# An attention and two-layer kernel on one core: w_in loaded in two pieces of eight column chunks, and the order of the first third of the work arranged anew

## The chip, the cores and the metric

The kernel runs on one core of one Trainium2 chip. The metric is the time of one execution on the device in microseconds (us), lower is better. The engines are called as in the profile: PE (TensorE, matrix products and transposes), DVE (VectorE), ACT (ScalarE), POOL (GpSimd) and SP (SyncE, which issues most of the transfers).

## The reference

A causal attention in which every query looks at the six best of 24 key chunks alone, and on its output two matrix products with an ELU between them:

```python
batch, n_heads, seq, head_dim = (4, 8, 768, 64)
chunk = 32; top_k = 6; scale = 1 / sqrt(64)
k_min, k_max = k_chunks.min(axis=3), k_chunks.max(axis=3)
ub = sum(maximum(q * k_min, q * k_max), axis=-1)          # a bound for each query and chunk
ub = where(causal, ub, -1e9)
top_chunks = argsort(ub, axis=-1)[..., -top_k:]
scores = where(selected & causal, scale * q @ k.T, -1e9)
attn = exp(scores - max) ; attn = attn / (sum(attn) + 1e-09)
x = (attn @ v) as [3072, 512]                              # tokens x (heads * 64)
h = x @ w_in                                               # w_in 512 x 2048
g = where(h > 0, h, exp(minimum(h, 0)) - 1)
out = g @ w_out                                            # w_out 2048 x 512
```

## The kernel before

The 3072 tokens are eight units of 384. Units 0 and 1 hold the first 192 tokens (tags with "p") and the next 192 (tags with "s") of batches 0 and 1 together; units 2 to 7 are the later half rows of batches 0 and 1 and the halves of batches 2 and 3. For each unit the kernel prepares keys and queries, selects chunks (not for the first 192 tokens, where all chunks are allowed), forms scores and attention, and turns the result into xt, four tiles of 128 channels x 384 tokens. Then comes that unit's layer.

The work is recorded as small steps with their reads and writes (`Graph`), and two long strings, ORDER and PLACES, give the order in which the steps are emitted, the engine of each one, and the buffer (one of 8 PSUM banks, one of 11 "f" buffers for loaded rows, and so on) of each tile. Nothing is rearranged afterwards: every engine, and every queue of transfers, goes through its steps in the order of that string, and waits in place where an input or a buffer is not ready.

The steps that the text below names:

- ldk, ldq, ldv (L304, issued by SP, two of ldk by ACT): loads of keys, queries and values. ldq0s00 and ldq0s10 are the two loads of queries for batch 0, unit "s", ldk0s00 and ldk0s10 those of its keys. Their rows are 64 floats, 256 bytes. ec (SP): a copy of a constant into the keys' tile.
- kT, qT (L402, PE): transposes of loaded rows into a bank, four of 96 x 128 each; kmin, kmax (L367, DVE) and ks0, ks1 (L370) make the bounds of chunks from them; kt, qt, qh, ka, qa (L320 on ACT, L322 on DVE and POOL) copy them on, qr (L344 and L342) is a ReLU of a query.
- tr, sc, ex, pv, rcp, on: mask, scores, exponential, product with values, reciprocal and division. ub, ubT, max, lt, sT, mk: the selection.
- px (L669, PE) and xt (L320 on ACT, L322 on DVE): the turned result, the layer's input.
- w_in0 and so on (L291), w_out0 to w_out3 (L297): the weights, loaded by POOL with a cast from float32 to bfloat16.
- h (L851, PE, four products of 128 x 384 for each of 16 column chunks), e (ACT, exponential), m (L860, POOL or DVE), g (DVE): the first product and the ELU. h0.4 is chunk 4 of unit 0; it needs all four xt and the piece of w_in that holds column chunk 4. o (L875, PE): the second product.
- vz, rz, oh, kq, tris, es: constants; kb, ky202: parts of keys' tiles for later batches.

On POOL the pieces stand in this order among the rest: oh, vz0, ka01p0, v0p1, rz, w_in1 (column chunks 4 to 7), v0p0, v1p0, w_in0 (chunks 0 to 3), ka10p0, ks1p1, w_in2 (chunks 8 to 15), and then with work between them w_out0 to w_out3. The layer of unit 0 starts with chunks 4, 6 and 5 accordingly, then qT0s0, chunk 3, qT0s1, chunks 2, 1, 7, the selection's ub00, chunk 0, and the upper eight.

A load of w_in is one call:

```python
def load_w_in(i, c0, c1):
    return g.op(f"w_in{i}", (POOL,),
                lambda e: nc.gpsimd.dma_start(out=w_in_sb[:, :, P * c0:P * c1],
                                              in_=wi[:, :, P * c0:P * c1]),
                writes=[(fixed, ("wi", fc)) for fc in range(c0, c1)], dma=True)
```

Its rows in the core's memory are 128 bfloat16 for each column chunk: 1 KB in the pieces of four chunks, 2 KB in the piece of eight.

Of the kernel before, what the change touches and what calls it, by code (L numbers as in the profile page):

```python
# [39 lines left out]
G0iS0WD01A02D09D06S0sG0kD0jG0aS0yD03D00D0qG0mG0bA0VG04D05G0eS0uG0cG0dA0tS0rS0vS0xD0lD0oS0wS0YS0X  # L40
P0MD0OD0QS0BP1oP0DP1aP11S0ZS0zD0ED0NA0HA0IG0fG0gD0FP0KP1pA1eG0pP1kA0LD1bP0TA0RA15A17G16P1jP1tP1l
S0+D0UP1qP1uD1cP18A1nD13S2gS2fG0CA1rP1hD19A1sG0nP1zD12S2hS2iP1yA1iP1AA1gA1mGmED0PA1CP1vA1xA1BG0A
P1DP26P25P1ED10G0-S2PS2vS2OD27D28D1FA1wP1YP20P2aGmDA0SP29D2bP1XA2cP1+D21G0JP1IP1OP1RP1SP1HS2IP2o
P1ND1GD1JD1ZD1KP2dG1dGmFA1-P1LD2qD1PA1QD2jD22P23D1TD1UD2eA2sD24A1MS2QP1VD1WG08G2uG0hP2BD2DD2CA2t
Pm-Pn6G2EAn7GbsGmGPn2Gn8D2pG2rAm+Dn0D14D0GAn3Dn4P2wPmWA2xA2yS2RP2JA2KDn5D2zPmSPmODn9Dn1AmXAmTD2L
GmYPnaGmHDmZAmPP3lAnbGmIA2FDmQDmUPmKAmLDmVD3nD3mA2MD3pGncPnGG2HPniA2AG07GmMA1fPnCG2SAnjD3oPnuD3q
D3rPnmDmRDmNG3tPneAnHA3sGnkDndAnvGnIP3HDnlAnDPnqGnwA3IDnJP41PnyDnxAnrA3uGnEDnFP3JP3+AnfPnQDnsS2k
A3KDntD2NAnnS3fG3LP2XA42P38PnRS2mA40GmJAnzA2GDnoD2ZDnpD2YP4lGngPnKPnXA4mD3vDnhA2+A30D43D3cP4DA4E
P4FG3ePnYA4GGnAD3aA3dD39D2-D31P4jD4HP3gG3bP33PnSS32S4+A34D35PnLA3hA4kD3iG3kS2TDnBP3wD4nS2VG2lG36
D3xG3jS50PnZPn-A2nD3yD3zA37S4-D3APnMPnTD3BD3CS4YD3GA3EG3FP3NDnUP4OP4MS4XS4ZP3MD3DP48P45A4PA4NP44  # L50
G2UG2WP4aD3ODn+D3PP4IP4JA4bP3SPnNA49D46D47A3TD4cS7UP3QD4QAnOP4sP4uP4dA3RP4eP4oS7SA4tP4pD4fP5rG3U
D4gA4vP4RD4KD4LP4SP4hA5sP5QS7WD4TD4UP3VP3WA5RD4qP5fP4VD3XD3YA5gS7RP5ED4rG4wP4xA4WP4yD5SP3ZA5FD4z
P58D4AA5iS57P5kD5aA4iP4BA4CG7VS53P5JD3-P5xD59G5TG5uA5cS55D5BA5oA5NPolPoJD5mA5GD5KPo5S5wAoKD5zS8l
PoxD5yGoLAo6SaND5LA5IPo9A5tDoMSo0G5bPodGo7AomD5lS51AoyG5MPohDo8G5nAoaSnPGonPoRA5OScZGobDooAoePoF
D7TA5hGofAoSPopDocG5AA5jGozDogPo1AoGGoTSnVDoAAoqPoBGoHDoUS7NAoiGorA5DPotDoIS7OAo2GojDosP5VAouGo3
DokA5HGovDo4A5UG5PDowA5vPoNAoCG5dD5XPp1A52G7XD5WAoOD5ZGoDPp2A5qGoPA5eD5YPpePpfD5-SnWPp7D5+SaHPp8
DoEA60G61DoQPpgD63A56DaOP66P6gA67P64DaQP6cP6iA65Pp3D62A6dDaPA6jP6mP68A6hP6lD5pP6aDaRP6eA6nPp9A69
D54SaSG6oA6fP6BP6xD6kPoVA6bS7MA6CP6vA6yS7YP6qA6wP6HS7PP6pAoWP6zA6IS7QPoZD6rGoXD6sA6AG5CP6JDoYAo-
P6tScRP6MGbmP6ND6uA6KP7bGo+P7cP76A6OP6-Dp0PphA77D6LA7dD6PShFScXG7eDaTP6FA6+Pp4ApiA6GP6DA6EP72P70
P78P6RDp5A71A79DaUP6QDaVA73P7CP74A75P6YA6ZP7xP7zA7yA7ADaWP7ZD7aD6SSb3P6WA6XPpaApbP7DSpjSp6G7BP8g  # L60
A8hD7-D81D6TD7+P7rP7lP7fP7gP7tP89P7pD8iA7EG7FD7hD7iD8aD8bG8kG8jP7vP8yD8zA7mA7sA7qA7uP7nA7oA7wP8m
P6UP8FP7GScSSaCDb4A8CD8DG8EA6VA8dG8fP7HD7ID7JA8qP7jA7kP84A85P8tA8uAaIA8vD8oP7KD7LPpkPpEPpQPpsPpM
# [48 lines left out]
61242021924655001a2670213436574570014300947225611670302352031120804001116121g0720201135240126206
7b02263110d23604056a1340210e012f31211457500812314c3642415207730642056120013310460542957032603134
12613204502065601021112331061123044022301072011211a322032100236151720be0251232130061652720cg4100
# [867 lines left out]
```

## Time and profile before

| | us |
|---|---|
| median of 3 runs (280.64 to 281.32) | 281.04 |
| the profiled execution | 281.25 |
| its span, first to last instruction | 279.5 |
| PE busy in the span | 263.2 (94%) |
| DVE busy | 217.4 (78%) |
| ACT busy | 217.1 (78%) |
| POOL busy | 125.5 (45%) |
| loads of w_in, issue to landing: two of 512 KB, median | 8.8 |
| load of w_in of 1024 KB, issue to landing | 13.6 |

The times in the views are counted from the first instruction of the span. "PE" rows give matrix products and transposes, "PEld" the loads of their stationary operands. A row of the view in order of time has start, duration, engine, line, operation, tiles and count; what stands in brackets is how long the engine was idle before it and what ended that. A row of a group has busy time and mean duration in ns, and then the idle time before its instructions. The rows of the transfers give queue, packets, MB and the share of 16 engines' time, or a load's tiles, count, size and the median from issue to landing; q0 is the queue that POOL fills, q1 the one that SP fills. The DMA share can exceed 1 because packets overlap on an engine.

### The profile page before, as it was taken

To read this page: it belongs to the slowest core of one execution; us is meant where nothing else is said; L and a number is where in the kernel's file an instruction comes from. 1 tells how busy PE (TensorE), PEld (TensorE's weight loads), DVE (VectorE), ACT (ScalarE), POOL (GpSimd) and SP (SyncE) were. 2 spreads that over 40 slices of the span, in tenths; PEclk is the share of its full clock that TensorE was granted. 3 is DMA by queue.
4 is the path that set the end of the run, shared out by engine and by line. 5 is a ranking of instruction groups with operands and counts; after the bars stand their busy time and mean duration, and the time that the engine had idled before them with its cause. 6 is when DMAs were issued, how large, how long until landed. Compare 5 with 4: busy or idle time off the path is not lost.

```text
span 279.5 us, 6918 instructions
## 1 busy us (share of the span) xinstructions
PE 263.2 (94%) x2436; PEld 162.9 (58%) x2436; DVE 217.4 (78%) x656; ACT 217.1 (78%) x493; POOL 125.5 (45%) x249
## 2 busy tenths in 40 slices
PE   1978899999999999999999999999999999999994
PEld 0745465785456755576555555666655556665553
DVE  4668978799978999979998999569797698424931
ACT  2596796789699998999999859886968579982620
POOL 8674745348521755422685736222541346310410
PEclk9999999999999999999999999999999999999999
DMA  8999999999529999946985499416600210042002
GB/s 163 198 211 211 199 211 210 217 202 251 123 60 203 247 219 230 196 115 112 171 203 114 109 226 206 84 36 136 170 4 0 60 39 1 16 139 82 15 17 96
DMA packets 103779, 38.47 MB, mean 138 GB/s; under 512 B 95168, under 2 KB 99520, under 8 KB 103744
## 3 DMA queue, kind: packets, MB, share of 16 engines
q1 hardware_dynamic: 98864, 33.53, 57.3%
q0 software_dynamic: 3696, 4.19, 8.7%
q10 hardware_dynamic: 1184, 0.30, 0.5%
q8 instruction: 19, 0.31, 0.5%
q14 instruction: 16, 0.13, 0.1%
HBM read 30.41 MB, written 6.29 MB: 131 GB/s over the span
## 4 chain that ended last, share of the span: by engine, by line
PE 70%; DVE 13%; DMA 8%; ACT 4%; issue 1%; POOL 1%; SPq 0%; DVEq 0%; ACTq 0%
PE bank L875 24%; PE bank L851 22%; PE bank L782 9%; DMA w_in_sb<-in_moe_w_in_dram 5%; PE bank L833 5%; DVE gT L864 2%; PE bank L592 2%; PE bank L402 2%; DMA kc<-in_k_dram 2%; ACT e L858 2%; DMA f<-in_k_dram 1%; PE bank L543 1%; PE bank L728 1%; PE bank L893 1%; DVE on L646 1%
## 5 line engine op out<-in xcount | busy, mean ns | idle before, releaser
L851 PE MATMUL bank<-xt,w_in_sb 128*128 128x384 bf16 x512 | 89.2, 326 | 2.2 <-DMA w_in_sb<-in_moe_w_in_dram 2.2
L875 PE MATMUL bank<-w_out_sb,gT 128*128 128x512 bf16 x368 | 89.5, 379 | 0.0
L860 POOL TENSOR_SCALAR m<-e 128x384 f32<-128x384 f32 x96 | 50.7, 536 | 59.3 <-ACT e L858 47.0
L864 DVE SCALAR_TENSOR_TENSOR gT<-bank,m 128x384 bf16<-128x384 f32 x128 | 65.9, 549 | 9.7 <-POOL m L860 8.4
L858 ACT ACTIVATE e<-bank 128x384 f32<-128x384 f32 x128 | 58.6, 493 | 16.7 <-PE bank L851 13.9
L851 PEld LDWEIGHTS <-w_in_sb 128*128 128x128 bf16 x512 | 49.1, 98 | 36.6 <-DMA w_in_sb<-in_moe_w_in_dram 3.0
L797 ACT ACTIVATE pt<-bank 128x384 bf16<-128x384 f32 (+1 forms) x144 | 67.0, 547 | 3.5 <-PE bank L782 2.1
L875 PEld LDWEIGHTS <-gT 128*128 128x128 bf16 x368 | 34.6, 97 | 35.7 <-issue 2.2
L782 PE MATMUL bank<-rhs,lhs 96*128 96x384 bf16 (+2 forms) x240 | 42.8, 293 | 1.0 <-DVE on L646 0.5
L814 POOL TENSOR_TENSOR pt<-pt,tri 128x256 bf16<-128x256 bf16 (+1 forms) x18 | 16.6, 924 | 39.3 <-ACT pt L801 20.1
L782 PEld LDWEIGHTS <-lhs 96*128 96x128 bf16 x240 | 21.7, 97 | 13.9 <-issue 0.9
L833 PEld LDWEIGHTS <-pt 128*128 128x128 bf16 x576 | 21.0, 97 | 4.0 <-DVE pt L814 0.4
L833 PE MATMUL bank<-vext,pt 128*128 128x65 bf16 x576 | 22.2, 193 | 0.3 <-DVE pt L814 0.3
L646 DVE TENSOR_TENSOR on<-bank,rcp 128x384 bf16<-128x384 f32 (+1 forms) x37 | 18.8, 509 | 1.2
L367 DVE TENSOR_REDUCE kst<-bank 128x12 f32<-128x384 f32 x32 | 16.6, 548 | 3.7 <-PE bank L402 2.8
L322 POOL CAST rhs<-qt 64x384 bf16<-64x384 f32 x23 | 12.3, 542 | 13.1 <-ACT qt L320 12.1
L636 DVE RECIPROCAL rcp<-bank 128x6 f32<-128x6 f32 (+1 forms) x40 | 7.3, 185 | 14.0 <-PE bank L833 8.7
L320 ACT ACTIVATE o<-bank 128x512 f32<-128x512 f32 (+1 forms) x13 | 7.5, 587 | 13.0 <-PE bank L875 10.1
L322 DVE COPY o<-bank 128x512 f32<-128x512 f32 (+1 forms) x12 | 7.9, 663 | 12.0 <-PE bank L875 10.0
L860 DVE TENSOR_SCALAR m<-e 128x384 f32<-128x384 f32 x32 | 13.1, 417 | 2.8 <-ACT e L858 2.6
L402 PE MATMUL bank<-ident_f,f 96*128 96x96 f32 x64 | 9.3, 295 | 6.2 <-DMA f<-in_k_dram 6.2
L814 DVE TENSOR_TENSOR pt<-pt,tri 128x512 bf16<-128x512 bf16 (+1 forms) x30 | 10.8, 376 | 5.3 <-ACT pt L801 3.5
(102 smaller groups left out, 338.6 us busy)
## 6 DMA issues: line engine op xcount, KB each, us to landing
f<-in_v_dram SPq DMA_DIRECT2D x22, 256.0 KB, 4.8
out_dram<-o SPq DMA_DIRECT2D x21, 256.0 KB, 3.4
f<-in_q_dram SPq DMA_DIRECT2D x18, 256.0 KB, 4.9
f<-in_k_dram SPq DMA_DIRECT2D x18, 256.0 KB, 4.7
kc<-in_k_dram SPq DMA_DIRECT2D x8, 384.0 KB, 4.3
w_out_sb<-in_moe_w_out_dram POOLq DMA_DIRECT2D x4, 512.0 KB, 10.5
f<-in_q_dram SPq DMA_DIRECT2D x6, 192.0 KB, 5.0
w_in_sb<-in_moe_w_in_dram POOLq DMA_DIRECT2D x2, 512.0 KB, 8.8
```

The lines of the kernel that those rows point to most:

```text
L322: eng[e].tensor_copy(out=dst, in_=src)
L367: g.op(("kmin", "kmax")[w] + tag, (DVE,), lambda e, w=w, op=op: nc.vector.tensor_reduce(out=cs(w), in_=src(), axis=AX.X, op=op), reads=[(b ...
L646: nc.vector.tensor_tensor(out=ap(on)[:, 0:nt].rearrange("p q h d -> p h q d"), in0=view()[:, :, :, 0:D], in1=ap(rcp)[:, :, 0:nt].to_broadc ...
L782: nc.tensor.matmul(ap(banks[hd])[:, o + pc:o + pc + wd], lhsT=apl(ls, G)[0:96, pr, hd, P * kb:P * (kb + 1)], rhs=ap(rs)[0:96, hd, c0 - HS ...
L797: lambda e, hd=hd, pt=pt, banks=banks, wtot=wtot: nc.scalar.activation(out=ap(pt)[:, hd, PAD:PAD + wtot], in_=ap(banks[hd])[:, 0:wtot], fu ...
L814: eng[e].tensor_tensor(out=view, in0=view, in1=tri[:, 64:64 + P].rearrange("p (a b w) -> p a b w", a=1, b=1) .to_broadcast([P, 2, len(dg), ...
L833: nc.tensor.matmul(view()[:, hd, qi, :], lhsT=ap(pt)[:, hd, P * qi + off:P * qi + off + P], rhs=ap(vx[b])[:, kb, 2 * r + hd, :], start=(kb ...
L851: nc.tensor.matmul(ap(bank)[:, 0:HS], lhsT=w_in_sb[:, kk, P * fc:P * (fc + 1)], rhs=ap(xT[i, kk]), start=(kk == 0), stop=(kk == NKK - 1))
L858: g.op(f"e{i}.{fc}", (ACT,), lambda e, eb=eb, bank=bank: nc.scalar.activation(out=ap(eb), in_=ap(bank)[:, 0:HS], func=AF.Exp), reads=[(ban ...
L860: g.op(f"m{i}.{fc}", (POOL, DVE), lambda e, eb=eb, mb=mb: eng[e].tensor_scalar(out=ap(mb), in0=ap(eb), scalar1=-1.0, scalar2=1.0, op0=AOT. ...
L864: nc.vector.scalar_tensor_tensor(out=ap(gt), in0=ap(bank)[:, 0:HS], scalar=0.0, in1=ap(mb), op0=AOT.max, op1=AOT.min),
L875: nc.tensor.matmul(ap(bank), lhsT=ap(gts[fc])[:, P * tt:P * (tt + 1)], rhs=w_out_sb[:, fc, :], start=(fc == 0), stop=(fc == NFC - 1))
```

## The change

w_in is loaded in two pieces: w_in0 holds column chunks 0 to 7, w_in1 chunks 8 to 15. Both have rows of 2 KB. The strings ORDER and PLACES are new in their first third: the order of the steps up to the middle of unit 2's preparation, the engine of 52 steps, and the buffers. From there on the order on each engine is the same as before (the last 500 of 604 steps on PE, the last 408 of 490 on ACT, 381 of 476 on DVE, 166 of 226 on POOL; SP's steps keep their order throughout). The work itself is the same; no step is added or left out but for the piece.

```diff
-    for i, (c0, c1) in enumerate(((0, 4), (4, 8), (8, 16))):
+    for i, (c0, c1) in enumerate(((0, 8), (8, 16))):
         load_w_in(i, c0, c1)
     for i in range(4):
         load_w_out(i)
...
 ORDER = """
-G0iS0WD01A02D09D06S0sG0kD0jG0aS0yD03D00D0qG0mG0bA0VG04D05G0eS0uG0cG0dA0tS0rS0vS0xD0lD0oS0wS0YS0X
...
+G0iS0WD01A02D09A0VG0kD06A0tS0sD0jG0aS0yG0mD03D00S0uD0qG0bS0rG04S0vG0eD05G0cS0xD0lG0dS0wD0oG0fS0Y
...
```

Read out of the strings, these are the orders on two engines from the constants to the first products of the layer:

```
POOL before: es0 es1 oh vz0 ka01p0 v0p1 rz w_in1 v0p0 v1p0 w_in0 ka10p0 ks1p1 w_in2 tris2 ka10s0 kq ks0s1 ky202 w_out0 m0.6 ks0s0 m0.3 w_out1 w_out2
POOL after:  es0 es1 tris2 oh ks0p0 ky202 kq vz0 w_in0 w_in1 w_out0 ks1p0 v1p1 vc0 qa00s0 ka00s0 ka11p0 ks0s1 ks0s0 m0.4 m0.6 m0.5 ks1p1 w_out1
PE before:   ... kT0s0 pv0p10 pxp3 pxp0 pxp2 pxp1 kT0s1 h0.4 h0.6 h0.5 qT0s0 h0.3 qT0s1 h0.2 h0.1 h0.7 ub00 h0.0 h0.15
PE after:    ... pv1p11 pv1p10 pxp3 qT0s0 pxp0 kT0s1 pxp2 qT0s1 kT0s0 pxp1 h0.4 h0.6 h0.5 h0.2 h0.3 h0.1 ub00 h0.7 h0.0 h0.15
```

On DVE the step rz now stands behind kmax0p0 and kmin0p0, on which ks0p0 waits; v1p0 is on DVE, v0p1, v0p0 and ka01p0 are on ACT. The order of the ACT steps around the layer's start is xtp0, qt0s0, xtp2, qt0s1, qr0s1, kt0s0, e0.4; on DVE kmin0s1, xtp1, xtp3, three reductions, g0.4.

More of the change, by code (lines that the diff above doesn't have):

```diff
@@ L45 @@
[L45 to L62, printed above, removed]
@@ new lines @@
+A1wP1HP1SP1RA1GS3fD2bD2cP2dD1JD1KG2jA22D1ZD1-P2wP1LP2BA1MA2xG2zD0PP23P2JP2oD1PD1TA24A2KA2LD1UD1Q
+D2CA2sG2tG17P1VD1WD2ePmZAm-S2mD2qD2pD2DG2ES32G2rGm+Pn5An6Pn1Dn0Gn7Dn8A0JA2yPmRPmVAn2PmNGn3Dn4AmS
+AmWDmXG1dGmGGmTDmYP3lD3mD3nAmOA0SGmPS4+Pn9PmJA2FG2HDmUA2uS2TG2NPnFAmKA2AD3oPntD3pD3qGmHGmLPnpAna
+AnuGnvDmQPnhD3rA2MGnbPnBDmMAniAnGG3sS2VDncGnjAnCDnwPnlPndA3tGmIDnkAnmP3HA3IDnDDnEPnxP41AnqGnHDnI
+P38D3aA42G2GP2XGnrDnsA3uP3JPnJA3KS50GnnDnoAneGnfP3+PnPPnWA40D2YD2ZDngD2+G2-A3cG3eAnyG07G3LP4lD39
+D43D3vP3gPnXA4mA30P4DP33A34G3bD3hG3jA3iPnKPnQS4-A36S4YD35DnzG2nP3wA4ES4XS4ZP4jP4FPnLPnRD3yD3xD3A
@@ new lines @@
+D3zA2lA4kG4nA31A37A4GD3BP3MP44P45P3NPnYD3CG3FA3EP4aDnAD3DS7UD3OP48G3GG3kD46D3dA4bS7SPnSA49A47G4c
+S7WD2SD3PP4MD2UPnZDn-A4NG2WP4OA4PS7RP3QP3SP4sDnTD4QS57A4tA3TA3RG3UPnMAnNP4oD4HS53P4pP4eP4dD4fP4u
+P4JA4vP4IP5rD4gG4wP4RD4KP4SA5sD4LP4hP5QD4TD4UP3VP3WA5RD4qP5fD3XP4VD3YA5gP5ED4rP4xA4WP4yG7VS55D5S
+P3ZA5FD4zP58D4AG5TA5iP5kS5wD5aA4iP4BG5uS8lP5JD3-A4CP5xD59SaNA5cPokD5BA5oPoIA5ND5mA5GD5KPo4Sn+AoJ
+D5zPowD5yGoKAo5D5LA5IG5bPo8S51Go6DoLA5tPocG5MD5lSnOAolAoxDo7PogScZG5nAo9GomPoQA5OGoaDonAodPoED7T
+A5hSnUGoeDobAoRPooS7NA5jG5ADofGoyPo0AoFS7OGoSDozAopPoAGoGDoTAohA5DPosGoqDoHAo1GoiDorP5VSnVAotGo2
@@ L112 @@
[L112 to L117 removed]
+012340567081020931a40252363471110201041552002113862247600753a62123141020130023514002651251013236
@@ L118 @@
+1617422270631425714655632103016030121042187512231010621b2000240dg1131522041c6170220621e120f04121
+531709062120
 """
```

115 lines of the change are left out of this document (60 added, 55 removed).

## The prediction

> **What bounds the kernel now.** I read the page's groups first, then the table by stages, then the waits, then the stretch that the change reorders instruction by instruction.
>
> ```profile
> PE 263.2 (94%) x2436; PEld 162.9 (58%) x2436; DVE 217.4 (78%) x656; ACT 217.1 (78%) x493; POOL 125.5 (45%) x249
> L851 PE MATMUL bank<-xt,w_in_sb 128*128 128x384 bf16 x512 | 89.2, 326 | 2.2 <-DMA w_in_sb<-in_moe_w_in_dram 2.2
> ```
>
> TensorE is busy 263.2 of 279.5 us, so what any reordering can win is the 16.3 us in which it idles. The stages say where that is:
>
> ```profile
> 10.00:20.00 10.00, 8.42 (x111) 5.73 (x110) 5.56 (x19) 8.55 (x23) 7.17 (x11) 1.00 1.33 196
> 20.00:30.00 10.00, 8.22 (x84) 4.97 (x85) 8.48 (x25) 7.42 (x21) 5.13 (x10) 1.00 1.18 217
> 30.00:40.00 10.00, 8.80 (x62) 5.34 (x61) 8.45 (x31) 7.96 (x17) 5.67 (x13) 1.00 1.21 198
> 40.00:50.00 10.00, 10.00 (x88) 5.36 (x87) 8.73 (x35) 6.37 (x14) 4.62 (x9) 1.00 1.20 217
> ```
>
> (Columns: stretch, length, busy time of PE, PEld, DVE, ACT, POOL, clock, DMA share, GB/s.) PE loses 1.6, 1.8 and 1.2 us in the first three and nothing in the fourth. The DMA share is over 1 and the rate stays near 200 GB/s throughout: in this stretch the DMA engines are full, and what one transfer wins another one loses. The waits that w_in causes, on PE:
>
> ```profile
> 22.40 2.12 PE L851 MATMUL bank<-xt,w_in_sb 128*128 128x384 bf16 x12
> 24.36 0.49 PE L402 MATMUL bank<-ident_f,f 96*128 96x96 f32 x4
> 25.89 0.82 PE L851 MATMUL bank<-xt,w_in_sb 128*128 128x384 bf16 x4 [1.04 <-DMA w_in_sb<-in_moe_w_in_dram]
> 31.75 1.47 PE L851 MATMUL bank<-xt,w_in_sb 128*128 128x384 bf16 x8 [1.19 <-DMA w_in_sb<-in_moe_w_in_dram]
> ```
>
> The first layer starts at 22.40, waits 1.04 us for the second piece and 1.19 us for the third: the 2.2 us of the group. These are all the change can remove directly.
>
> **When the pieces are issued.** GpSimd issues w_in, in its own order. In the changed order nothing but small things stands ahead of it: es0, es1, tris2, oh, ks0p0, ky202, kq, vz0, then both pieces and w_out0 at once; rz, ka01p0, v0p1, v0p0 and v1p0, which stood in between, went to DVE and ACT.
>
> ```profile
> 5.67 0.26 POOL L282 MEMSET onehot<- 128x192 bf16 x1
> 5.99 3.10 POOL L285 MEMSET onehot<- 32x1 bf16 x24
> 9.15 0.53 POOL L247 MEMSET vext<- 64x520 bf16 x1
> 14.12 0.98 POOL L291 DMA_DIRECT2D w_in_sb<-in_moe_w_in_dram  x1
> 18.86 0.25 POOL L263 TENSOR_SCALAR_AFFINE_SELECT tri<-tri 128x64 bf16<-128x64 bf16 x1
> 22.49 0.63 POOL L247 MEMSET kt<- 128x640 bf16 x1
> 23.68 0.21 POOL L370 TENSOR_TENSOR kst<-kst 128x12 f32<-128x12 f32 x1 [0.55 <-DVE kst L367]
> 24.06 0.40 POOL L322 COPY kt<-onehot 128x256 bf16<-128x256 bf16 x1 [0.17 <-PE bank L851]
> 8.41 1.67 DVE L367 TENSOR_REDUCE kst<-bank 128x12 f32<-128x384 f32 x3
> ```
>
> oh ends at 9.09, with tris2 ahead of it at 9.35. ks0p0 needs two of the reductions that start at 8.41, done near 9.45. Then 0.21 + 0.40 + 0.63 + 0.53 = 1.77: w_in0 is issued at 11.2 instead of 14.12, 2.9 us earlier, w_in1 near 12.2, w_out0 near 13.
>
> **What an early w_in does to SyncE's loads.** The DMA view, a few stretches. First all that SyncE had issued by 13.85, and what its queue had moved:
>
> ```profile
> q1 hardware_dynamic: 8863, 2.21, 102.2%
> f<-in_q_dram SPq DMA_DIRECT2D x4, 192.0 KB, 4.6
> f<-in_k_dram SPq DMA_DIRECT2D x3, 192.0 KB, 4.6
> f<-in_v_dram SPq DMA_DIRECT2D x2, 256.0 KB, 5.1
> f<-in_q_dram SPq DMA_DIRECT2D x4, 96.0 KB, 4.0
> f<-in_k_dram SPq DMA_DIRECT2D x3, 96.0 KB, 4.1
> f<-in_v_dram SPq DMA_DIRECT2D x2, 128.0 KB, 4.9
> ```
>
> That is 2784 KB = 2.85 MB issued, the last of it ldq0s10 (queries of the second unit, batch 0). 0.64 MB are still queued at 13.85. Now stretches 0:18, 14:16, 17:19, 24.5:30 and 30.5:33.8; q0 is GpSimd's queue, q1 SyncE's (queue, packets, MB, share):
>
> ```profile
> q0 software_dynamic: 199, 0.20, 6.9%
> ...
> q1 hardware_dynamic: 1626, 0.41, 137.3%
> f<-in_q_dram SPq DMA_DIRECT2D x1, 192.0 KB, 5.1
> ...
> f<-in_q_dram SPq DMA_DIRECT2D x2, 192.0 KB, 21.0
> ...
> q0 software_dynamic: 511, 0.98, 94.1%
> q1 hardware_dynamic: 512, 0.15, 18.7%
> ...
> q0 software_dynamic: 496, 0.51, 89.7%
> q1 hardware_dynamic: 498, 0.13, 28.9%
> ```
>
> Alone, q1 moves 0.41 MB in 2 us (0.205 MB/us). Beside w_in2, whose packets are 2 KB, the two queues take turns packet by packet, 511 to 512: q0 gets 0.98 MB in 5.5 us (0.178 MB/us), q1, whose packets are 256 bytes, 0.15 MB (0.027 MB/us). Beside w_out (1 KB packets) q0 gets 0.155 and q1 0.04 MB/us. So while a weight is on its way SyncE's loads nearly stand still: two loads issued at 18 to 19 us took 21.0 us (median) where 5 is usual. In the kernel before, ldq0s10 (issued 13.24, 5.1 us, landed 18.3) slipped through just ahead: w_in's first 199 packets by 18.0 put its start at about 16.8, 2.7 us after its issue.
>
> In the changed kernel q0 starts at 11.2 + 2.7 = 13.9, with the 0.64 MB still queued: most of ldk0s10, all of ldk0s00, ldq0s00 and ldq0s10. q0 then holds w_in0 (1.05 MB, 5.9 us), w_in1 (5.9 us) and w_out0 (0.52 MB, 3.4 us) without a break, to 29.1. In that time q1 gets 0.16 + 0.16 + 0.13 = 0.45 MB. The last 0.19 MB take 0.9 us alone: 30.0. Before, 0.64 MB from 13.85 on at 0.205 would be out at 17.0, against 18.3 landed; I add 1.2 us likewise: **ldq0s10 lands at 31.2**.
>
> **Who waits for it.** In the changed order PE has qT0s0 (transposes of ldq0s00 and ldq0s10) right behind pxp3, and behind it pxp0, kT0s1, pxp2, qT0s1, kT0s0, pxp1 and the whole first layer; before, qT0s0 stood behind three products of it. PE executes in order. ACT (xtp0), DVE (xtp1, xtp3) and POOL (qa00s0, and behind it w_out1 to w_out3) wait in turn. From 31.2 to the first product of the layer: 15 transposes L402, 12 transposes L669, then two copies of xt on DVE.
>
> ```profile
> 7.73 2.56 PE bank L402 x16
> 44.12 0.66 PE bank L402 x8
> 56.08 0.22 PE bank L669 x4
> 21.64 0.88 DVE L322 COPY xt<-bank 128x384 bf16<-128x384 bf16 x3
> ```
>
> The chain of waits gives 0.66/8 = 0.0825 and 0.22/4 = 0.055 each: 15 x 0.0825 + 12 x 0.055 = 1.9, and 2 x 0.29 = 0.6, in all 2.5. The layer starts at 33.7 instead of 22.40: +11.3. From there on both pieces are present, so the 2.2 us of waits are gone, and the 8 transposes of qT0s0 and qT0s1 (0.66) that lay behind 22.40 are done: 11.3 - 2.9 = **+8.4**.
>
> **A cold TensorE.** The same rows show that transposes took 2.56/16 = 0.16 us each at the start and 0.0825 later, though the granted clock stands at 1.00. The views of the kernel before show no PE gap over 1.2 us once it is under way, so no row shows what an 11 us gap does; bounds 0 (nothing) and 2.7 (all slow for the 6 us that it lasted at the start: the 1.9 us of transposes doubled, then 1.6 us of half-rate products). I take 2.0, near the upper, as the start is itself a case of PE after idling. The Trainium skill (TensorE: Matmul & The Clock Gate, What's actually happening) says that the array falls to half clock after an idle window of about 3.4 us and needs as long to come back, which I would estimate as 1.7 us here. By that the sum would be 0.3 lower; the granted clock in the rows does not show the gate at all.
>
> **What costs nothing.**
>
> ```profile
> L860 POOL TENSOR_SCALAR m<-e 128x384 f32<-128x384 f32 x96 | 50.7, 536 | 59.3 <-ACT e L858 47.0
> ```
>
> The order on SyncE's queue is the same as before, and every engine's order is identical from the last third of unit two on. 52 small steps change engine, among them three net of the layer's m to POOL (13 instead of 10, 0.54 us each). PE needs 16 x 0.65 = 10.4 us for the layer's products (12 of them take 2.12 with the last one's tail, 0.163 each, four a step); POOL's 13 m's, 7.0 us, with some 4 us of copies and issues between, just fit. Without that cover it would be 0.5 us per m. Nothing later gains in what is seen here: PE has no idle time from 40 to 50 to give back. w_out1 to w_out3 are issued 11 us late like their readers.
>
> Sum: 281.25 (the profiled execution; span 279.5) + 8.4 + 2.0 = 291.65, less 0.2 for the median (281.04): **291.4**.
>
> **Rivals.**
> *A, the forecast:* the q loads starve. The sum hangs little on when q0 starts: a start 0.5 us later sends 0.1 MB more ahead, and the end of q0 moves back as much. L between 29 and 33, the cold term between 0 and 2.7: 287 to 294.
> *B, partly starved.* If q0's packets start 2 us later than I think (POOL is held up, or a transfer of 2 KB rows is slower to begin), the backlog is at most 0.25 MB and drains beside w_in: L = 23 to 28. At L = 25.5 the layer starts at 28.0, +5.6 - 2.9 = +2.7, time 283.7; range 281.5 to 287. For it: the 2.7 us rest on a single start on an empty queue. Against: the only wait ahead of w_in0 on POOL is ks0p0's.
> *C, faster.* The loads keep their pace. It decides whether the two queues share by bytes or by packets while 2 KB packets run. By bytes, 1.05 + 0.64 MB at 0.2 MB/us put w_in0 at 13.9 + 8.4 + 1.2 = 23.5 and w_in1 before it is needed; h0.4 comes 1.1 later, 2.9 are saved: 281.04 - 1.8 = 279.2. Against it stands 511 to 512. The Trainium skill (DMA: Bandwidth & Descriptors, Rules for kernel authors) would have transfers of 1 MiB and more for bandwidth, which speaks for C; the rows agree in size (0.178 against 0.155 MB/us) but show who pays.
>
> **Chances.** A 0.72, B 0.14, C 0.14. A run of this kernel can tell 0.2% (0.6 us) from no change. Faster: C and a sliver of B, 0.15; same 0.02; slower 0.83. The range reaches from the middle of B to the upper end of A: 283 to 294.5.
>
> **What would show it.** POOL's first L291 near 11.2; the q loads issued at 12.31 and 13.24 landing near 30 instead of 17 to 18; a gap of about 11 us on PE ahead of an L402, ended by DMA f<-in_q_dram; the first L851 near 34 to 36 with no later wait for w_in; L402 at 0.16 us behind the gap (or 0.08, then the cold term is wrong). Wrong if qT0s0 runs before 24.

## The result and the profile after

The changed kernel takes 293.26 us (median of 4 runs, 292.96 to 293.88), the kernel before 280.95 us (4 runs, 280.64 to 281.32): a ratio of 1.0434, with a 95% interval of 1.0417 to 1.045. It is 12.3 us slower; 291.4 had been forecast, in a range of 283 to 294.5. The profiled execution of the changed kernel took 293.52 us, its span 291.8.

The page of the changed kernel, its engine row, the two groups that matter and the row of the clock:

```profile
PE 266.4 (91%) x2436; PEld 165.5 (57%) x2436; DVE 215.3 (74%) x645; ACT 220.3 (75%) x498; POOL 125.9 (43%) x254
L851 PE MATMUL bank<-xt,w_in_sb 128*128 128x384 bf16 x512 | 89.0, 326 | 0.3 <-DVE xt L322 0.3
L402 PE MATMUL bank<-ident_f,f 96*128 96x96 f32 x64 | 12.3, 343 | 18.7 <-DMA f<-in_q_dram 12.3
PEclk9995599999999999999999999999999999999999
```

The first-stage products of the layer (L851) no longer wait for w_in at all: the 2.2 us of the group are now 0.3 us, for a copy. Instead the transposes (L402) wait 12.3 us for the query loads, and the clock stands at half in two of the 40 slices. The same place on PE, instruction by instruction:

```profile
19.62 0.39 PE L669 MATMUL bank<-ident_b,on 128*128 128x128 bf16 x4
26.70 0.39 PE L402 MATMUL bank<-ident_f,f 96*128 96x96 f32 x1 [6.70 <-DMA f<-in_q_dram]
32.71 0.74 PE L402 MATMUL bank<-ident_f,f 96*128 96x96 f32 x3 [5.61 <-DMA f<-in_q_dram]
...
34.74 1.49 PE L402 MATMUL bank<-ident_f,f 96*128 96x96 f32 x8
36.02 0.63 PE L669 MATMUL bank<-ident_b,on 128*128 128x128 bf16 x4
36.45 0.42 PE L851 MATMUL bank<-xt,w_in_sb 128*128 128x384 bf16 x1
37.17 3.90 PE L851 MATMUL bank<-xt,w_in_sb 128*128 128x384 bf16 x23 [0.31 <-DVE xt L322]
```

From 20.0 to 32.71 PE does one transpose. The one at 26.70 is released by ldq0s00, the three at 32.71 by ldq0s10. The layer starts at 36.45, before at 22.40. The trace has w_in0 landed at 21.80 and w_in1 at 28.70, so the first piece lies ready for 14.6 us.

Why the loads are late is in the DMA view of the changed kernel, stretch 18 to 24 (queue, packets, MB, share):

```profile
q0 software_dynamic: 544, 1.08, 94.9%
q1 hardware_dynamic: 543, 0.14, 17.5%
```

One packet of 2 KB from GpSimd's queue, one of 256 bytes from SyncE's, in turn: 0.18 MB/us for w_in, 0.023 MB/us for all of SyncE's loads together. The chain of waits has it as one piece, the longest of the execution:

```profile
13.36 19.31 DMA f<-in_q_dram
32.67 0.04 issue
32.71 0.74 PE bank L402 x3
33.45 0.43 PE bank L669 x4
33.88 0.64 PE bank L402 x4
```

And the clock that was granted, in the table by stages (stretch, length, busy time of PE, PEld, DVE, ACT, POOL, clock, DMA share, GB/s):

```profile
16.20:22.90 6.70, 3.42 (x71) 2.46 (x68) 2.72 (x13) 4.81 (x15) 0.13 (x1) 1.00 1.13 205
23.00:32.70 9.70, 0.39 (x1) 0.18 (x1) 0.00 (x0) 0.00 (x0) 0.00 (x0) 0.50 1.17 212
32.70:36.60 3.90, 3.89 (x28) 3.86 (x29) 1.31 (x3) 2.31 (x6) 0.50 (x1) 0.50 1.04 189
36.70:60.00 23.30, 22.72 (x199) 13.12 (x198) 19.60 (x66) 19.22 (x42) 16.60 (x33) 1.00 1.03 186
```

Some 3 us after PE's work ends at 20.0 the clock is halved, and it comes back 3.9 us after the transposes resume. In those 3.9 us a transpose costs 0.16 us (0.64/4 in the chain), twice the usual.

### The profile page after: what moved, and what is told of

Read it like the earlier page. It is cut to its first block, busy times and chain, and to the rows that moved or that the text cites. A ratio compares the mean times of both kernels' runs of the same rounds, so it can differ in the third digit from the quotient of the medians.

```text
span 291.8 us, 6918 instructions
## 1 busy us (share of the span) xinstructions
PE 266.4 (91%) x2436; PEld 165.5 (57%) x2436; DVE 215.3 (74%) x645; ACT 220.3 (75%) x498; POOL 125.9 (43%) x254
## 4 chain that ended last, share of the span: by engine, by line
PE 66%; DVE 16%; DMA 10%; ACT 2%; issue 2%; POOL 2%; SPq 0%; DVEq 0%; ACTq 0%; POOLq 0%
PE bank L875 22%; PE bank L851 20%; PE bank L782 8%; DMA f<-in_q_dram 7%; PE bank L833 4%; DVE gT L864 4%; PE bank L543 2%; PE bank L592 2%; PE bank L402 2%; DVE kst L367 2%; DMA kc<-in_k_dram 2%; DMA f<-in_k_dram 1%; POOL m L860 1%; ACT e L858 1%; DVE thr L611 1%
## 5 line engine op out<-in xcount | busy, mean ns | idle before, releaser
L851 PE MATMUL bank<-xt,w_in_sb 128*128 128x384 bf16 x512 | 89.0, 326 | 0.3 <-DVE xt L322 0.3
L860 POOL TENSOR_SCALAR m<-e 128x384 f32<-128x384 f32 x99 | 52.0, 533 | 59.1 <-ACT e L858 45.4
L851 PEld LDWEIGHTS <-w_in_sb 128*128 128x128 bf16 x512 | 49.4, 98 | 34.8 <-issue 3.3
L402 PE MATMUL bank<-ident_f,f 96*128 96x96 f32 x64 | 12.3, 343 | 18.7 <-DMA f<-in_q_dram 12.3
L402 PEld LDWEIGHTS bank<-ident_f,f 96*128 96x128 f32 x64 | 9.6, 203 | 21.0 <-issue 7.6
L320 ACT ACTIVATE xt<-bank 128x384 bf16<-128x384 bf16 (+1 forms) x12 | 5.9, 488 | 13.5 <-PE bank L669 13.1
```

Source lines behind the costliest of these rows:

```text
L402: nc.tensor.transpose(ap(bk)[:, c0:c0 + T96], ap(src[j])[0:T96, 256 * G + P * pr:256 * G + P * pr + P], ident_f[0:T96, 0:T96])
L851: nc.tensor.matmul(ap(bank)[:, 0:HS], lhsT=w_in_sb[:, kk, P * fc:P * (fc + 1)], rhs=ap(xT[i, kk]), start=(kk == 0), stop=(kk == NKK - 1))
L860: g.op(f"m{i}.{fc}", (POOL, DVE), lambda e, eb=eb, mb=mb: eng[e].tensor_scalar(out=ap(mb), in0=ap(eb), scalar1=-1.0, scalar2=1.0, op0=AOT. ...
```

## The experiments

The theory: w_in, issued early, takes the DMA engines packet by packet from the loads that qT0s0 needs; PE, in order, stands behind qT0s0; the idle array then runs at half clock for a while. The rivals: the two pieces are bad in themselves, the new order of the other work is, or it is the amount of bytes ahead and not the packets. Twelve kernels, each beside the kernel before on the same chip (the last column is the 95% interval of the ratio):

| kernel | what it is | us, median (runs) | before | ratio |
|---|---|---|---|---|
| e1 | changed, w_in issued 3.4 us later | 283.75 (10) | 281.05 | 1.0051 to 1.0104 |
| e2 | changed, rows of 256 bytes | 291.96 (4) | 281.17 | 1.0351 to 1.0409 |
| e3 | changed, PE kept busy in the gap | 292.04 (4) | 281.05 | 1.0369 to 1.0407 |
| e4 | before, two pieces of eight | 282.67 (4) | 281.05 | 1.0048 to 1.0082 |
| e5 | e1, PE kept busy in its wait | 282.34 (10) | 281.17 | 1.0028 to 1.0057 |
| e6 | changed, q transposes behind the layer on PE | 288.36 (4) | 281.17 | 1.0230 to 1.0271 |
| e7 | before, pieces issued back to back | 281.03 (12) | 281.17 | 0.9980 to 1.0008 |
| e8 | changed, three pieces | 290.85 (4) | 281.74 | 1.0270 to 1.0350 |
| e9 | changed, w_in issued 1.3 us later | 287.55 (4) | 281.74 | 1.0162 to 1.0245 |
| e10 | e1, three pieces | 284.43 (6) | 281.24 | 1.0067 to 1.0121 |
| e11 | e10 with products of zeros | 287.30 (4) | 281.24 | 1.0188 to 1.0232 |
| e12 | e1, three pieces, the needed one first | 281.91 (12) | 281.14 | 1.0011 to 1.0039 |

**The issue alone, later (e1).** On POOL:

```diff
-... vz0 w_in0 w_in1 w_out0 ks1p0 v1p1 vc0 ...
+... vz0 ks1p0 v1p1 w_in0 w_in1 w_out0 vc0 ...
```

> The changed kernel, with w_in0, w_in1 and w_out0 moved back on GpSimd behind v1p1, so about 3.5 us later; all other orders stay as changed. Starvation theory: GpSimd's queue then starts near 18.6, when the four q loads for qT0s0 have landed, so PE has no gap ahead of qT0s0, w_in0 lands near 25.4 and the layer starts there without a later wait for w_in: 281 us (280 to 282.5). Rival, the pieces of eight or the new order of the other work cost the 12 us by themselves: 289 or more.

Measured: 283.75. The loads landed at 17.5 and 18.4, qT0s0 ran at 19.74 without a gap, and nearly 10 of the 12.3 us are gone (1.0434 against 1.0077): the early issue is the cause. The rest of the expectation missed by 2.7 us. Timeline of PE, e1:

```profile
22.14 0.40 PE L669 MATMUL bank<-ident_b,on 128*128 128x128 bf16 x4
25.84 5.47 PE L851 MATMUL bank<-xt,w_in_sb 128*128 128x384 bf16 x24 [3.30 <-DMA w_in_sb<-in_moe_w_in_dram]
```

The layer starts at 25.84, near the expected 25.4, but 24 products take 5.47 us where 12 took 2.12: behind a wait of 3.3 us, too, the clock is halved. One of the ten runs had a mean clock of 1.000, and it took 281.15 us; the nine others had 0.988 to 0.994 and took 283.24 to 284.3. (The mean alone is weak evidence, since it does not say where the clock was low: the kernel before has runs with a mean of 0.988 to 0.994 that take no longer than its others. The next experiment decides it.)

**The same with PE kept busy (e5).** The products of zeros are the step that the kernel uses elsewhere to keep PE busy; their bank is h0.4's, which overwrites it.

```diff
-PE: ... pxp1 h0.4 ...
+PE: ... pxp1 [28 x fill] h0.4 ...
```

> The later issue of the first runs (w_in0, w_in1, w_out0 behind v1p1), with 28 products of zeros on PE right ahead of h0.4, 0.11 us each, which fill the wait for w_in0 (3.3 us) nearly to its end and go to the bank that h0.4 then overwrites. w_in0 lands near 25.8 as before. Clock theory: what that kernel lost to the kernel before, beyond the later start, is the half clock behind the wait (24 products in 5.47 us instead of 4.0); with PE kept busy it does not come: 281.8 us (281 to 282.5). Rival, the clock has nothing to do with it: 283.7 again, or more by what the fills overrun.

Measured: 282.34, all ten runs at a clock of 0.997 to 1.000. Timeline of PE, e5:

```profile
22.63 3.22 PE L932 MATMUL bank<-zeros 128*128 128x256 bf16 x28
25.68 4.06 PE L852 MATMUL bank<-xt,w_in_sb 128*128 128x384 bf16 x24
```

The layer starts hardly earlier (25.68 against 25.84), but its first 24 products take 4.06 us instead of 5.47. The difference of 1.4 us is that of the medians (283.75 against 282.34). Half clock behind the wait is shown.

**PE kept busy in the changed kernel's gap (e3).**

```diff
-PE: ... pv1p10 pxp3 qT0s0 ...
+PE: ... pv1p10 pxp3 [105 x fill] qT0s0 ...
```

> The changed kernel with 105 products of zeros on PE right ahead of qT0s0 (they end before the loads land, and go to the bank that qT0s0 then overwrites). The loads starve as before, so the gap's end stays at 32.7. Clock theory: PE stays at full clock through the gap, the transposes behind it take 0.083 us each instead of 0.16, the layer starts 1.5 to 2 us earlier: 291.5 us (290.8 to 292). Rival, the slow transposes have another cause, or what they lose is hidden: 293.3.

Measured: 292.04, just over the upper end of the expectation, against 293.26 for the changed kernel. Timeline of PE, e3:

```profile
19.70 11.62 PE L936 MATMUL bank<-zeros 128*128 128x256 bf16 x105 [0.28 <-ACT on L648]
31.16 0.25 PE L407 MATMUL bank<-ident_f,f 96*128 96x96 f32 x1
31.79 0.47 PE L407 MATMUL bank<-ident_f,f 96*128 96x96 f32 x3 [0.38 <-DMA f<-in_q_dram]
...
32.88 0.83 PE L407 MATMUL bank<-ident_f,f 96*128 96x96 f32 x8
...
34.45 3.90 PE L856 MATMUL bank<-xt,w_in_sb 128*128 128x384 bf16 x23 [0.31 <-DVE xt L327]
```

Eight transposes take 0.83 us instead of 1.49, and from the last load's landing to the row of 23 products it is 34.45 - 31.74 = 2.7 us instead of 37.17 - 32.67 = 4.5: half clock cost 1.8 us at this place. In the whole time less of it is seen: 1.2 us between the medians, and between the two profiled executions 2.3 us (293.52 against 291.18), of which 0.93 are the load itself, which landed that much earlier, and no edit explains that.

**The packets made equal (e2).**

```diff
-w_in_sb = const.tile([P, NKK, DFF], BF16, name="w_in_sb")
+w_in_sb = const.tile([P, NKK, NFC, P + 2], BF16, name="w_in_sb")
...
-nc.gpsimd.dma_start(out=w_in_sb[:, :, P * c0:P * c1], in_=wi[:, :, P * c0:P * c1])
+for kk in range(NKK):
+    nc.gpsimd.dma_start(out=w_in_sb[:, kk, c0:c1, 0:P],
+                        in_=wi[:, kk, P * c0:P * c1].rearrange("p (c w) -> p c w", w=P))
...
-lhsT=w_in_sb[:, kk, P * fc:P * (fc + 1)]
+lhsT=w_in_sb[:, kk, fc, 0:P]
```

> The changed kernel at the same place in the order, but w_in is written into rows of 256 bytes (the tile padded by two columns per chunk, one transfer for each of the four k slices), so that its packets are as small as those of SyncE's loads. Nothing else changes; GpSimd needs eight issues instead of two. Packet theory: the queues then share by halves, ldq0s10 lands near 21 instead of 32.7, w_in0 near 24 to 26.5, which then starts the layer (and, by the first runs, a wait of over 2 us halves the clock for a while): 286 us (283 to 289). Rival, it is the amount of bytes ahead or the order that starves the loads, not the size of a packet: ldq0s10 lands near 30 again, 292 or more.

Measured: ldq0s10 landed at 22.1, near the 21 of the packet theory and far from its rival's 30, but the time was 291.96, some 6 us over what I expected. DMA view of e2, stretch 29 to 31:

```profile
q0 software_dynamic: 676, 0.17, 83.5%
q1 hardware_dynamic: 676, 0.17, 64.6%
```

Packet for packet again, and now byte for byte; so it is from 19 on, while ldq0s10 is on its way. (Between 18 and 19 SyncE's queue moved only 67 packets to 588 of GpSimd's; these runs do not say why.) What I had not reckoned with is that both queues together move 170 GB/s so, and w_in gets half of it. Timeline of PE, e2:

```profile
20.89 2.20 PE L756 MATMUL bank<-vext,pt 128*128 128x65 bf16 x37 [3.52 <-POOL vext L335]
...
28.23 3.59 PE L853 MATMUL bank<-xt,w_in_sb 128*128 128x384 bf16 x21 [1.08 <-DMA w_in_sb<-in_moe_w_in_dram]
...
37.28 0.34 PE L853 MATMUL bank<-xt,w_in_sb 128*128 128x384 bf16 x1 [2.83 <-DMA w_in_sb<-in_moe_w_in_dram]
40.54 4.88 PE L853 MATMUL bank<-xt,w_in_sb 128*128 128x384 bf16 x15 [2.92 <-DMA w_in_sb<-in_moe_w_in_dram]
```

The weights are what is late now (w_in1 lands at 40.5), and a cast waits behind the eight issues on POOL, which costs PE the 3.52 us at 20.89. The mechanism is shown by the landing and the packets; the time alone would have spoken for the rival.

**Who waits (e6).** qT0s0, qT0s1 and all that needs them (their copies, ub00, the selection, the first scores) are put behind h0.13 on every engine; two banks and the buffers of some later loads change with it.

```diff
-PE: ... pxp3 qT0s0 pxp0 kT0s1 pxp2 qT0s1 kT0s0 pxp1 h0.4 ... h0.1 ub00 h0.7 ... h0.13 ...
+PE: ... pxp3 pxp0 kT0s1 pxp2 kT0s0 pxp1 h0.4 ... h0.1 h0.7 ... h0.13 qT0s0 qT0s1 ub00 ...
```

> The changed kernel with w_in issued just as early, but qT0s0, qT0s1 and all that needs them (their copies, ub00, the selection, the first scores) put behind the layer's last first-stage product h0.13 on every engine. The loads starve as in the changed kernel (ldq0s10 lands near 32). Order theory: starving the loads costs only because PE, which executes in order, stands ahead of them; here the layer starts near 22.5, waits about 1 us for w_in1, and the q transposes come at 34 without a gap of their own: 285 us (282 to 288). Rival, the loads that are late cost the time wherever their readers stand, since the attention of the second unit behind them is what runs out: 290 or more.

Measured: 288.36, above the 282 to 288 and below the rival's 290. Timeline of PE, e6:

```profile
22.10 0.33 PE L851 MATMUL bank<-xt,w_in_sb 128*128 128x384 bf16 x1
22.71 10.89 PE L851 MATMUL bank<-xt,w_in_sb 128*128 128x384 bf16 x63 [0.29 <-DVE xt L322]
33.44 0.49 PE L402 MATMUL bank<-ident_f,f 96*128 96x96 f32 x4
...
40.84 0.60 PE L728 MATMUL bank<-rhs,lhs 96*128 96x128 bf16 x6 [3.58 <-POOL rhs L322]
```

The loads starved as before (ldq0s10 at 31.7), yet the whole first stage of the layer ran from 22.10 without a wait. That gives back 4.9 us. The other 7 stay: the selection of the second unit starts only at 33.4, PE waits 3.58 us for its end at 40.84 and has half clock behind that (from 41.4 to 48.3). So the late loads cost part of the time wherever their readers stand.

**A dose in between (e9).** On POOL, w_in0, w_in1 and w_out0 between ks1p0 and v1p1: issued at 13.43, against 12.09 in the changed kernel and 15.47 in e1.

```diff
-... vz0 w_in0 w_in1 w_out0 ks1p0 v1p1 vc0 ...
+... vz0 ks1p0 w_in0 w_in1 w_out0 v1p1 vc0 ...
```

> The changed kernel with w_in0, w_in1 and w_out0 behind ks1p0 on GpSimd, issued near 13.05: 1 us later than in the changed kernel, 2.4 us before the later issue of the first runs. The queue then starts near 16.1 with some 0.26 MB of SyncE's loads ahead of the end of ldq0s10. Beside w_in0 (5.9 us) 0.16 MB leave, the last 0.1 take 3.7 us beside w_in1: ldq0s10 lands near 27, the layer starts near 30.5 with the cold clock: 287 us (285 to 289). If instead a small backlog drains before the weights get going: 282 to 284, as with the later issue; if the place matters little once it is ahead of the loads: 292.

Measured: 287.55, ldq0s10 at 26.65. Timeline of PE, e9:

```profile
19.48 0.30 PE L402 MATMUL bank<-ident_f,f 96*128 96x96 f32 x1 [0.28 <-ACT on L643]
26.70 0.74 PE L402 MATMUL bank<-ident_f,f 96*128 96x96 f32 x3 [6.92 <-DMA f<-in_q_dram]
```

ldq0s00 is through in time, only the last load, ldq0s10, is held up for 7 us: 0.25 MB are still queued when w_in's first packet moves at 15.8. The rule by which the expectation was made (what is queued when w_in's packets start, over the rate beside them) gave 27 and 287.

**Three pieces at the early place (e8).**

```diff
-for i, (c0, c1) in enumerate(((0, 8), (8, 16))):
+for i, (c0, c1) in enumerate(((0, 4), (4, 8), (8, 16))):
...
-POOL: ... vz0 w_in0 w_in1 w_out0 ...
+POOL: ... vz0 w_in0 w_in1 w_in2 w_out0 ...
```

> The changed kernel with w_in in three pieces again (chunks 0 to 3, 4 to 7, 8 to 15), issued one behind the other at the same early place; all else stays. By the rates: 0.47 MB of SyncE's loads are queued when GpSimd's queue starts at 15.06; beside two pieces with rows of 1 KB (3.4 us each, 0.04 MB/us for SyncE) 0.27 MB of it leave, beside w_in2 (5.9 us, 0.027) 0.16, the rest beside w_out0: ldq0s10 lands near 30 instead of 32.7, the layer starts as much earlier: 291 us (290 to 292.5). Rival, the two pieces of eight are what costs and three are well: 283 or less.

Measured: 290.85, ldq0s10 at 30.19. DMA view of e8, stretch 18 to 24:

```profile
q0 software_dynamic: 818, 0.98, 92.5%
q1 hardware_dynamic: 815, 0.20, 26.1%
```

With rows of 1 KB in part of the stretch SyncE's loads get 0.20 MB instead of 0.14. The number of pieces is worth 2.4 us by the medians and 3.5 by the ratios (1.0434 against 1.0310), and ldq0s10 lands 2.5 us earlier; it isn't the cause of the 12.

**Two pieces in the kernel before (e4).**

```diff
-((0, 4), (4, 8), (8, 16))      POOL: ... w_in1 v0p0 v1p0 w_in0 ka10p0 ks1p1 w_in2 ...
+((0, 8), (8, 16))              POOL: ... w_in0 v0p0 v1p0 ka10p0 ks1p1 w_in1 ...
```

(The expectation counts the places by the old names: chunks 0 to 7 go where w_in1 stood, which the kernel before issues first, at 14.12; chunks 8 to 15 where w_in2 stood; w_in0's place is left out. All else is in the old order.)

> The kernel before, every order as it was, with w_in in two pieces of eight: w_in0 (0 to 8) at the place of its second piece, w_in1 (8 to 16) at that of its third, the first place left out. Starvation theory: the first piece starts after ldq0s10 has landed, the layer starts some 1.5 us later than with a piece of four but has no wait for the second piece: 280.5 us (279.5 to 281.5). Rival, two pieces with rows of 2 KB are bad in themselves: over 284.

Measured: 282.67, 2 us over the expectation, and well under the rival's 284. Timeline of PE, e4:

```profile
21.08 0.76 PE L402 MATMUL bank<-ident_f,f 96*128 96x96 f32 x4
24.31 3.93 PE L851 MATMUL bank<-xt,w_in_sb 128*128 128x384 bf16 x12 [2.47 <-DMA w_in_sb<-in_moe_w_in_dram]
```

The layer starts at 24.31, 0.4 us later than expected, and the waits behind it are gone. But its first 12 products take 3.93 us, against 2.12: 1.8 us of the 2 is half clock. The wait for the larger first piece, which begins at 21.84, can't be its whole reason, as the clock fell at 21.2 already (the rows are in the last section).

**The new order of the other work alone (e10, e11, e12).** e1 with three pieces; in e10 in the order 0 to 3, 4 to 7, 8 to 15, in e11 with 20 products of zeros ahead of h0.15, in e12 with 4 to 7 first, as the kernel before has them.

```diff
-POOL: ... v1p1 w_in0 w_in1 w_out0 vc0 ...
+POOL: ... v1p1 w_in0 w_in1 w_in2 w_out0 vc0 ...        (e10, e11)
+POOL: ... v1p1 w_in1 w_in0 w_in2 w_out0 vc0 ...        (e12)
...
-PE: ... h0.0 h0.15 ...
+PE: ... h0.0 [20 x fill] h0.15 ...                     (e11)
```

> Only the third part of the change is left: the new order of all other work, with w_in in its old three pieces and issued late enough (behind v1p1, near 15.4, w_out0 behind them). No load starves. The first piece lands near 22.6, when PE has done the transposes, so the layer starts there; the second is needed near 25.3 and lands near 25.7; the third lands near 31.5, as the DMA queue holds as many bytes ahead of it as in the kernel before, and h0.15 waits some 2.5 us for it, which may halve the clock. If the order itself is as good as the old one: 281 to 282.5, most likely 281.8, since h0.15 starts where it did before. If the order costs by itself: 283.5 or more with no wait that explains it. If it gains: under 280.5.

Measured: 284.43. The expectation overlooked that h0.4, the first step of the layer, needs chunk 4, the second piece here. Timeline of PE, e10:

```profile
26.75 5.63 PE L851 MATMUL bank<-xt,w_in_sb 128*128 128x384 bf16 x24 [3.59 <-DMA w_in_sb<-in_moe_w_in_dram]
```

So the layer waited for 1 MB as in e1, with half clock behind the wait, and there was no wait ahead of h0.15. e10 therefore says nothing of the order; e12 does.

> The same with 20 products of zeros ahead of h0.15 (2.2 us, in its wait for the third piece, into the bank that it then overwrites), so that PE does not idle there. If a wait of 2.5 us halves the clock: 0.5 to 1.3 us less than without them, near 281. If it does not: the same time.

Measured: 287.30, 2.9 us more than e10 and 6 over the expectation, which had been made on the same wrong reading. With no wait where they stood, the products of zeros cost their own 2.35 us and some. It is a check on e3 and e5: there they were free and gained, because they stood in a wait.

> Again only the new order of all other work, with three pieces issued behind v1p1, but chunks 4 to 7 first, which h0.4, h0.6 and h0.5 need, then 0 to 3, then 8 to 15, as the kernel before issues them. No load starves. The layer starts near 22.8 instead of 26.75, h0.2 waits about 1 us for the second piece, h0.15 some 2 us for the third, which lands near 31.5 to 32.5 as it did in the last two runs. If the new order costs nothing by itself, the time is that of the kernel before plus what the third piece lands later than its 31.7: 281.0 to 282.5, most likely 281.6. If the order costs: 283 or more though no load is late and the layer starts at 22.8.

Measured: 281.91, as expected. Timeline of PE, e12:

```profile
23.48 2.12 PE L851 MATMUL bank<-xt,w_in_sb 128*128 128x384 bf16 x12 [1.17 <-DMA w_in_sb<-in_moe_w_in_dram]
26.88 2.12 PE L851 MATMUL bank<-xt,w_in_sb 128*128 128x384 bf16 x12 [1.28 <-DMA w_in_sb<-in_moe_w_in_dram]
...
32.72 4.72 PE L851 MATMUL bank<-xt,w_in_sb 128*128 128x384 bf16 x28 [1.49 <-DMA w_in_sb<-in_moe_w_in_dram]
```

Three waits of 1.2 to 1.5 us, and full clock behind each (12 products in 2.12). In this execution (283.09 us, at the upper end of the kernel's runs) the third piece lands 0.97 us later than in the kernel before (32.72 against 31.75). That would be enough for the 0.8 us by which the medians differ, but where the piece lands in the run of the median isn't known, so this isn't shown. What the new order costs by itself is at most the 0.4% of the interval, 1.1 us.

**The old order, pieces back to back (e7).** An attempt to beat both kernels.

```diff
-POOL: ... rz w_in1 v0p0 v1p0 w_in0 ka10p0 ks1p1 w_in2 tris2 ...
+POOL: ... rz w_in1 w_in0 w_in2 ka10p0 ks1p1 tris2 ...        (v0p0 and v1p0 on DVE)
```

> The kernel before, its three pieces of w_in issued one right behind the other at the place of the first (14.1, 15.1, 15.9 instead of 14.1, 16.5, 18.1), with v0p0 and v1p0, which stood between them on GpSimd, on DVE. The q loads are out by then as before. If the DMA queue has no break between the first two pieces, w_in0 lands about 1 us earlier and w_in2 near 30.7 instead of 31.7: the wait of 1.04 us goes, the one of 1.19 stays: 280.0 us (279.5 to 280.8). Rival, the queue's rate is taken up already and the pieces land as before, or the two casts on DVE delay the products that need them: 281 to 282.

Measured: 281.03 against 281.17, no difference, as the rival has it, though not for its reason. Timeline of PE, e7:

```profile
25.30 0.82 PE L851 MATMUL bank<-xt,w_in_sb 128*128 128x384 bf16 x4 [0.50 <-DMA w_in_sb<-in_moe_w_in_dram]
...
31.05 4.07 PE L851 MATMUL bank<-xt,w_in_sb 128*128 128x384 bf16 x24 [1.07 <-DVE ubT L609]
```

The second piece comes 0.6 us earlier and the third 0.7 (the wait at 31.05 is put down to DVE, but w_in2 landed at 31.00). 0.5 us of it is left in the span of the profiled execution (279.0 against 279.5); the medians show none of it. Whether it is lost on the way or drowned in the spread of the runs (280.38 to 281.74) isn't settled. No kernel of this study beats the one before.

## Why the prediction was right, point by point

The sign, the place and the mechanism held: the loads of qT0s0 starve behind w_in, PE stands behind qT0s0, and no later wait for w_in is left. Of rival C (sharing by bytes) nothing is left: 544 packets to 543. Rival B was wrong in its price. e9 is its case, with w_in issued 2.2 us after the 11.2 of the prediction; ldq0s10 came at 26.65, near B's 25.5, but the time is 287.55 and not 283.7, just above the 287 at which its range ended: the layer starts at 30.43 and not 28.0. Of these 2.4 us the load's landing is 1.15, and the rest is the half clock (23.7 to 30.5 in e9), which B left out.

The terms, in the profiled executions:

| term | predicted | measured |
|---|---|---|
| w_in0 issued | 11.2 | 12.09 |
| GpSimd's queue moves its first packet | 13.9 | 15.06 |
| queued for SyncE then | 0.64 MB | 0.47 MB |
| w_out0, the last weight, is through | 29.1 | 30.5, all but 0.01 MB (landed 32.4) |
| ldq0s10 landed | 31.2 | 32.67 |
| from there to the layer, warm, and the cold clock | 2.5 + 2.0 | 2.7 + 1.8 |
| the layer runs from | 35.7 | 37.0 |
| given back behind it | -2.9 | -2.3 |
| time against before | +10.4 | +12.3 |

*The issue* came 0.9 us later, because ks0p0's second reduction was. Timelines of DVE and of POOL in the changed kernel:

```profile
9.71 0.56 DVE L367 TENSOR_REDUCE kst<-bank 128x12 f32<-128x384 f32 x1 [0.56 <-ACT kt L320]
```

```profile
10.43 0.22 POOL L370 TENSOR_TENSOR kst<-kst 128x12 f32<-128x12 f32 x1 [1.10 <-DVE kst L367]
...
12.09 1.75 POOL L291 DMA_DIRECT2D w_in_sb<-in_moe_w_in_dram  x2
```

I had taken the start of the reductions from the old order, in which copies on ACT stand elsewhere.

*The landing* came 1.5 us later than forecast. The rate beside 2 KB packets was a little lower (0.14 MB in 6 us, 0.023 MB/us, where 0.027 had been taken); still, SyncE's queue had moved the 0.47 MB by 30.2, against 30.0 in the prediction. From there to the landing it took 2.5 us, where 1.2 had been added: in 30.5 to 32 GpSimd's queue still moves a few packets of w_out0, 18 in all, so a small part of the transfers runs late; the link between the two isn't shown. This term is the larger part of the 1.9 us by which the sum fell short.

That the sum hung little on the start of GpSimd's queue was luck. It holds only while more is queued for SyncE than leaves beside the weights, 0.45 MB by the prediction's own rates; the run stood at that edge, with 0.47. In e9 the queue starts at 15.8, 0.8 us later than in the changed kernel, with 0.25 MB queued, and ldq0s10 lands 6.0 us earlier: beside the weights 0.25 MB take 10.9 us there, 0.47 MB take 17.6 us here. So rival B's case was under a microsecond away.

*From the landing to the layer* the working held: 4.5 us, of which 2.7 are there with a warm array (e3) and 1.8 are the half clock, put at 2.0 between 0 and 2.7. The rule that was set against that value, from the Trainium skill (TensorE: Matmul & The Clock Gate, What's actually happening), gave 1.7; both are as near as these runs can tell (the whole time shows 1.2 to 1.8). The prediction's sentence that the granted clock does not show the gate was wrong: the rows of the changed kernel show 0.50 from 23.0 to 36.6, and those of the kernel before had 0.98 in its last 20 us. It holds for the start of the execution alone, where transposes take 0.16 us too and the rows of both kernels say 1.00. (One product runs at 36.45, ahead of the copies; the row of 23 at 37.17, so the layer counts from 0.16 before that.)

*Given back* were 2.3 us (the layer 14.6 us later, the end 12.3), not 2.9. The two waits for w_in and the moved transposes did go: from the layer's start to the end PE is busy 0.6 us less than before (248.7 against 249.3). But it idles 6.1 us where it idled 7.8, so of the 2.2 us of waits 1.7 are gained; 0.3 of the rest is a new wait for a copy on DVE ahead of L728, and 0.16 is the way the layer's start is counted.

So with the same two pieces the early issue costs 9.5 us by the medians and 10.0 by the ratios, its half clock included (the changed kernel against e1); with three pieces it is 8.9 and 8.0 (e8 against e12). e1 has a loss of its own that the changed kernel does not have: 1.4 us of half clock behind its wait for w_in0 (e1 against e5). Against e12, which differs from the changed kernel in the place and the pieces of w_in and in w_out0's place, the changed kernel loses 11.4 us by the medians. The 0.8 us that e12 still loses are the new order of the other work or the later landing of the last part of w_in; which of them isn't settled.

## What to carry to other kernels

Before a transfer is issued earlier, look at what another queue still has to bring for the next step in an engine's order, and at the packet sizes of both: beside 2 KB packets a queue of 256-byte packets fell to about a ninth of its rate, and a load that was queued behind took 13 to 19 us instead of 5. Here its landing came within 1.5 us of the forecast, made from the bytes queued at the start of the large transfer and the two rates, read from a stretch of the old trace where both queues are busy. But once the backlog leaves beside the large transfer, the landing hangs much on the start: 0.8 us of it moved the landing by 6.0 us between the changed kernel and e9. Once PE was under way, a wait of 2.8 us or more without products of zeros in it had half clock beside or behind it in each profiled execution; where its cost was measured, it was 1.2 to 1.8 us. Products of zeros in the wait took that back, though only as long as the wait was there.

## What the runs showed of the hardware

The halving of the clock comes in steps. Read from the table by stages in stretches of 0.5 us, a stretch of half clock lasts 3.4 us in e1, e10 and e11, 6.8 us in e4, e6, e9 and twice in e2, and 13.7 us in the changed kernel and e8: one, two and four times 3.4 (a stretch that the end of the execution cuts off is left out). The Trainium skill (TensorE: Matmul & The Clock Gate, What's actually happening) has a free-running window of 3.4 us, at whose ends the clock changes. These lengths agree with it, and so does the varying time between the start of a wait and the fall of the clock: 2.8 us in e1, 3.0 in the changed kernel, 3.9 in e9, and in e11 the fall comes 0.6 us after the wait of 2.80 us has ended.

The wait need not be as long as that. Table by stages, e4:

```profile
21.00:21.30 0.30, 0.30 (x6) 0.30 (x5) 0.30 (x2) 0.30 (x2) 0.06 (x1) 0.80 1.16 207
...
21.90:23.90 2.00, 0.00 (x0) 0.00 (x0) 1.49 (x3) 0.00 (x0) 0.96 (x3) 0.50 1.13 205
24.00:28.00 4.00, 3.69 (x12) 1.85 (x13) 0.01 (x1) 0.87 (x2) 1.06 (x2) 0.50 1.13 207
28.00:40.00 12.00, 12.00 (x110) 7.41 (x108) 11.49 (x41) 10.52 (x24) 6.84 (x15) 1.00 1.23 211
```

Here the wait is 2.47 us, from 21.84 on, and the clock stands at half already as it begins, behind a stretch in which PE was busy some 60% of the time (1.82 of the 3.1 us from 18.0 on). The kernel before has such a stretch too (1.98 of 3.2 us), and there the clock stays full in the profiled execution. All four runs of e4 had a mean clock of 0.987 or 0.988, which is what 6.8 us of half clock in the 281 us make. In e12 waits of 1.2 to 1.5 us left it full. Where between them the border is, and how much the work ahead of the wait counts, these runs do not tell.
